# Wide weight pieces spread over the experts' slots: fewer of them in the first ten

## The chip, the cores and the metric

The kernel runs on one NeuronCore of one Trainium2 chip. The metric is the time of one execution on the device in microseconds (us), lower is better. A core has five engines that run their own instruction queues in order and meet at semaphores: the tensor engine (PE) for matrix products, VectorE (DVE), ScalarE (ACT), GpSimd (POOL) and SyncE (SP), which here issues nearly all transfers (DMA). Tiles live in on-chip memory (SBUF), matmul results in PSUM.

## What is computed

Three stages, one after the other, over 1536 tokens of width 512. First attention in 16 heads with a mask by hash buckets, then a mixture of 8 experts in which each token goes to one expert, then a layer with a softmax-like activation and a normalization. The change lies in the second stage and prepares the third:

```python
# experts: every token is computed by the expert e with its largest logit
h = np.maximum(x[mask] @ w1[e], 0.0)          # 512 -> 1024
ye = h @ w2[e]                                # 1024 -> 512
out[mask] = gate_w[mask, None] * eom[mask, e, None] * ye

# last stage
h = x @ w_in                                  # 512 -> 1024
e = np.exp(h - np.max(h, axis=-1, keepdims=True))
solu = h * (e / (np.sum(e, axis=-1, keepdims=True) + 1e-09))
ln = (solu - mu) / np.sqrt(var + 1e-06) * g_ln
out = ln @ w_out                              # 1024 -> 512
```

`w_in` and `w_out` of the last stage arrive as 64-bit floats; all other inputs have 32 bits.

## The kernel before

Every product is computed from 16-bit halves: a number is split into a high half and the rest (low half), and three matmuls (high by high, high by low, low by high) stand for one.

**The expert stage** is a list of 64 slots, written out by the loop over `slots`. A slot is one quarter of one of an expert's two products: 24 matmuls (`mm1` for the first product, `mm2` for the second). The order by blocks of four slots is m1 of expert 0, m1 of 1, m2 of 0, m1 of 2, m2 of 1, m1 of 3, m2 of 2, and so on: m1 of expert e+2 stands behind m2 of expert e. So slots 12 to 15 are m1 of expert 2, 16 to 19 m2 of expert 1, 44 to 47 m1 of expert 6, 60 to 63 m2 of expert 7. The columns of a matmul are the expert's places for tokens: 224, 224, 224, 212, 200, 192, 184, 168 from the fullest expert to the emptiest.

**What is queued in a slot**, in this order: ScalarE makes the high half of one piece of an expert's weights (`w_hi`, L142, 128x1024), VectorE the low half of the piece of the slot before (`w_lo`, L146), SyncE starts the load of the piece three slots ahead (`w_load`, L156 and L158), then whatever the table `todo` holds for the slot, then `run_late`, then the slot's matmuls and their evacuation. Slots 4 to 47 and 52 to 55 have such an expert piece. The raw pieces go through five buffers (`raw`), which VectorE's low half frees. In the third slot of an m1 block SyncE also issues the transposing load of a later expert's tokens (`x_load`, L1037).

**Evacuation.** After m1, ScalarE writes the hidden values twice (L1115, L1117) and GpSimd subtracts (L1118, `hh<-hf,hh`). After every second m2 slot ScalarE writes the high half of `yT` (L1147) and VectorE the low half (L1148); the latter is queued by `run_late` in the next slot, behind that slot's `todo`. PSUM has four buffers for these results (`ps_a`): a slot of m1 takes one, two slots of m2 share one. Each is given back by the instructions that evacuate it, for m2 by L1148.

**The wide pieces.** The 64-bit weights of the last stage come in 16 pieces of 512 KB, 0 to 7 from `w_in`, 8 to 15 from `w_out`. The kernel has no 64-bit arithmetic, so it decodes a piece with integer instructions, 128x512 each. `wide_a` has ScalarE's L122 and VectorE's L123, L125 and L126; `wide_b` is VectorE's L131; then ScalarE makes the high half (L142, `wi` or `wo`) and VectorE the low half (L146). The table `WD` names the slot of `wide_a` for each piece; `wide_b`, the high and the low half follow one, two and three slots later. The first five pieces are loaded before the stage, the others are issued by SyncE three slots ahead of `wide_a` (L110). They share five buffers (`raww`), and the decoded values two (`db`).

**The last stage** takes 12 tiles of 128 tokens: `h2` (L1262, 24 matmuls), then VectorE's and ScalarE's work of `solu_a` to `solu_d`, and four tiles later `outp` (L1329). What `todo` still holds for slots 64 and up is emitted here, two slots for each tile, ahead of that tile's work.

Of the kernel before, what the change touches and what calls it, by code (L numbers as in the profile page):

```python
# [21 lines left out]
def kernel(  # L22
# [903 lines left out]
    with tc.manual_schedule():  # L926
# [259 lines left out]
                f(*a)  # L1186


        WD = [0, 2, 4, 6, 8, 14, 20, 26] + [37 + 4 * x for x in range(8)]
        for x in range(16):  # L1190
            i = WD[x] if wide else 3 + 3 * x
            if wide:
# [16 lines left out]
        for i, (kd, e, g) in enumerate(slots):  # L1209
# [18 lines left out]
            if kd == "m2" and 4 * e + g < NTILE:  # L1228
# [4 lines left out]
                x = nc.gpsimd.indirect_dma_start(  # L1233
                    out=meta[:, :], out_offset=bass.IndirectOffsetOnAxis(ap=po, axis=0),
                    in_=me[:, t], in_offset=None).ins
# [150 lines left out]
```

## Time and profile before

| | before |
|---|---|
| median of 3 runs | 554.01 us |
| lowest and highest | 552.87 and 557.27 us |
| the profiled execution | 556.92 us, its span 555.1 us |
| mean granted clock of the tensor engine | 0.985 |
| PE busy | 518.3 us (93%) |
| VectorE busy | 395.9 us (71%) |
| ScalarE busy | 342.0 us (62%) |
| GpSimd busy | 257.7 us (46%) |
| expert stage, first to last slot | about 264 to 416 us of the span |

The span runs from the first to the last instruction. Busy time is the time in which an engine has an instruction under way. Matmuls are pipelined, so a busy tensor engine is not one at its peak. Averages over the span hide the stage that the change touches: the rows below are read there.

### The profile page before, as it was taken

What the parts mean: (1) busy time and instruction counts of PE and PEld (TensorE: products, weight loads), DVE (VectorE), ACT (ScalarE), POOL (GpSimd) and SP (SyncE); (2) the same over time, 40 slices, a digit from 0 to 9 for tenths busy, and PEclk for the clock granted to TensorE, in tenths of its full rate; (3) what the DMA queues carried; (4) which work ended last, traced back from release to release, by engine and by line L of the source; (5) the groups of instructions that cost most, each with busy time, mean ns of one, the idle gap of its engine ahead of it and who ended that gap; (6) DMA issues with size and microseconds to landing.
All of it is one profiled execution on the core that took longest, in us unless ns stands there. A gap on an engine that the chain in (4) does not pass through costs nothing. (4 is left out here: it accounts for less than half of the span.)

```text
span 555.1 us, 10812 instructions
## 1 busy us (share of the span) xinstructions
PE 518.3 (93%) x3900; PEld 351.5 (63%) x3900; DVE 395.9 (71%) x893; ACT 342.0 (62%) x642; POOL 257.7 (46%) x324
## 2 busy tenths in 40 slices
PE   6789999999999999999997989988999899999993
PEld 5446566666656655667996979987994344444441
DVE  7757777777777787766799987689995875645620
ACT  6677777877867777863386766587643453433420
POOL 7949493939696764716147546232220011121122
PEclk9999999999999999999998989998999999999998
DMA  5584977654839244304777999999600244243271
GB/s 170 109 222 105 225 151 221 151 155 103 230 82 222 90 92 132 91 1 170 234 219 144 330 225 262 235 341 342 243 3 2 43 85 100 58 89 83 57 113 58
DMA packets 107177, 83.13 MB, mean 150 GB/s; under 512 B 80624, under 2 KB 89456, under 8 KB 107120
## 3 DMA queue, kind: packets, MB, share of 16 engines
q1 hardware_dynamic: 104816, 76.09, 53.3%
q0 software_dynamic: 2304, 6.31, 3.2%
q8 instruction: 32, 0.52, 0.4%
q14 instruction: 25, 0.20, 0.1%
HBM read 51.43 MB, written 9.97 MB: 111 GB/s over the span
## 5 line engine op out<-in xcount | busy, mean ns | idle before, releaser
L566 ACT ACTIVATE p<-s,mx 128x768 f32<-128x768 f32 x96 | 95.2, 992 | 51.1 <-DVE mx L555 42.1
L551 DVE TENSOR_REDUCE mx<-s 128x1 f32<-128x768 f32 x96 | 91.7, 955 | 47.9 <-PE s L541 45.9
L580 PE MATMUL t<-ident,p 128*128 128x128 f32 x576 | 124.9, 274 | 0.7 <-ACT pt L582 0.7
L582 ACT COPY pt<-t 128x384 f32<-128x384 f32 x192 | 84.6, 478 | 10.8 <-PE t L580 9.5
L580 PEld LDWEIGHTS t<-ident,p 128*128 128x128 f32 x576 | 77.8, 141 | 15.3 <-ACT pt L582 5.0
L599 PE MATMUL v<-pt,v 128*64 128x384 f32 (+1 forms) x384 | 80.1, 503 | 0.9 <-DVE xt L626 0.9
L1118 POOL TENSOR_TENSOR hh<-hf,hh 128x448 f16<-128x448 f32 (+5 forms) x32 | 40.2, 1259 | 80.1 <-ACT hf L1117 80.1
L1262 PE MATMUL h<-wi,yT 128*128 128x512 f16 x288 | 65.8, 386 | 4.2 <-DVE so L1288 2.6
L1107 PE MATMUL a<-xw,wa 128*128 128x224 f16 (+5 forms) x224 | 57.3, 259 | 9.8 <-DVE yT L1148 8.8
L1138 PE MATMUL a<-hh,wb 128*128 128x224 f16 (+5 forms) x256 | 63.7, 252 | 0.0
L1139 PE MATMUL a<-hh,wb 128*128 128x224 f16 (+5 forms) x256 | 63.6, 251 | 0.0
L1140 PE MATMUL a<-hh,wb 128*128 128x224 f16 (+5 forms) x256 | 63.5, 251 | 0.0
L1329 PE MATMUL o<-wo,zT 128*128 128x512 f16 x288 | 63.5, 379 | 0.0
L541 PE MATMUL s<-k,q 128*128 128x384 f16 x192 | 58.3, 330 | 4.1 <-ACT p L566 4.1
L541 PE MATMUL s<-b,cm 128*128 128x384 f16 x192 | 57.2, 326 | 2.3 <-DVE b L510 1.1
L1109 PE MATMUL a<-xw,wa 128*128 128x224 f16 (+5 forms) x224 | 57.5, 260 | 1.4 <-DVE wa L146 1.4
L1108 PE MATMUL a<-xw,wa 128*128 128x224 f16 (+5 forms) x224 | 57.4, 259 | 0.0
L1262 PEld LDWEIGHTS <-yT 128*128 128x128 f16 x288 | 28.2, 99 | 40.3 <-DVE so L1288 3.8
L1329 PEld LDWEIGHTS <-zT 128*128 128x128 f16 x288 | 28.2, 98 | 34.0
L541 PEld LDWEIGHTS <-q 128*128 128x128 f16 x192 | 19.0, 99 | 39.7 <-issue 37.7
L1277 ACT ACTIVATE ex<-h,st,csc 128x1024 f32<-128x1024 f32 x12 | 14.4, 1203 | 43.3 <-DVE st L1300 32.6
L1301 POOL TENSOR_TENSOR st<-st,nhalf 128x2 f32<-128x2 f32 x12 | 8.5, 707 | 68.6 <-DVE st L1300 68.6
(255 smaller groups left out, 1017.7 us busy)
## 6 DMA issues: line engine op xcount, KB each, us to landing
raw<-in_moe_w_dram SPq DMA_DIRECT2D x64, 512.0 KB, 5.8
raww<-in_moe_w_in_dram SPq DMA_DIRECT2D x8, 512.0 KB
raww<-in_moe_w_out_dram SPq DMA_DIRECT2D x8, 512.0 KB, 6.9
xs<-raw SPq DMA_DIRECT2D x8, 448.0 KB
v<-in_v_dram SPq DMA_DIRECT2D x8, 384.0 KB
q<-in_q_dram SPq DMA_DIRECT2D x7, 384.0 KB, 3.8
k<-in_k_dram SPq DMA_DIRECT2D x7, 384.0 KB, 5.5
cm<-q SPq DMA_DIRECT2D x14, 96.0 KB, 2.1
```

The costliest lines, as they stand in the source:

```text
L541: nc.tensor.matmul(t[:, c, 0:SB], d[x, h][:, s], flat(d[y, h])[:, c * SB:(c + 1) * SB], start=first, stop=not first)
L551: nc.vector.tensor_reduce(out=mx[:, 0:1], in_=t[:, :, 0:SB], op=ALU.max, axis=AX.XY)
L566: nc.scalar.activation(out=p, in_=s_t.pop(i)[:, :, 0:SB], func=AF.Exp, scale=mx[:, 1:2], bias=mx[:, 2:3], accum_out=sums[j][:, qt, h:h + 1])
L580: nc.tensor.transpose(t[:, g * 128:(g + 1) * 128], p[:, c, g * 128:(g + 1) * 128], ident)
L582: nc.scalar.copy(out=pt[j, h][:, 3 * c:3 * c + 3, qt * 128:(qt + 1) * 128], in_=t[:, 0:SB].rearrange("p (g c) -> p g c", g=3))
L599: nc.tensor.matmul(pv[j, q0][64 * h:64 * h + 64, 0:w], vt[:, h, c], pt[j, h][:, c, q0 * 128:q1 * 128], start=(c == 0), stop=(c == NS - 1), ...
L1109: nc.tensor.matmul(ps[:, i, 0:n], w[:, 1, kk, fs], xw[:, kk], start=False, stop=(kk == KD - 1))
L1138: nc.tensor.matmul(ps, w[:, 0, f, ds], hh[:, 0, f], start=(f == 0), stop=False)
L1139: nc.tensor.matmul(ps, w[:, 0, f, ds], hh[:, 1, f], start=False, stop=False)
L1140: nc.tensor.matmul(ps, w[:, 1, f, ds], hh[:, 0, f], start=False, stop=(f == KF - 1))
L1262: nc.tensor.matmul(ps[:, c], yT[:, a, kk, ts], w_i[:, w, kk, c * 512:(c + 1) * 512], start=(kk == 0 and a == 0 and w == 0), stop=(kk == KD ...
L1329: nc.tensor.matmul(ps, zT[:, KF * a + f], w_o[:, w, f], start=(f == 0 and a == 0 and w == 0), stop=(f == KF - 1 and a == 1))
```

## The change

The table that gives each wide piece its slot is replaced. The old one has the first parts of pieces 0 to 7 at slots 0, 2, 4, 6, 8, 14, 20 and 26 and those of 8 to 15 at every fourth slot from 37 to 65. The new one has them at 0, 2, 10, 14, 18, 22, 26 and 30, and then at every fourth slot from 35 to 63. Nothing else differs.

```diff
-        WD = [0, 2, 4, 6, 8, 14, 20, 26] + [37 + 4 * x for x in range(8)]
+        WD = [0, 2, 10, 14, 18, 22, 26, 30] + [35 + 4 * x for x in range(8)]
```

The instructions of the tensor engine and of GpSimd keep their order. On VectorE, in slots 5 to 8 of the program before, the low halves of expert 2's first weights (`wa<-raw,wa`) alternate with the parts of pieces 1 to 4 (`raww` is a raw wide piece, `db` and `dm` its decoded values, `wi` the weights of the last stage):

```order
L146 SCALAR_TENSOR_TENSOR wa<-raw,wa 128x1024
L146 SCALAR_TENSOR_TENSOR wi<-db,wi 128x512
L131 SCALAR_TENSOR_TENSOR db<-dm,db 128x512
L146 SCALAR_TENSOR_TENSOR wa<-raw,wa 128x1024
L123 TENSOR_SCALAR db<-raww 128x512
L125 SCALAR_TENSOR_TENSOR db<-raww,db 128x512
L126 SCALAR_TENSOR_TENSOR db<-raww,db 128x512
L146 SCALAR_TENSOR_TENSOR wa<-raw,wa 128x1024
L146 SCALAR_TENSOR_TENSOR wi<-db,wi 128x512
L131 SCALAR_TENSOR_TENSOR db<-dm,db 128x512
L146 SCALAR_TENSOR_TENSOR wa<-raw,wa 128x1024
L123 TENSOR_SCALAR db<-raww 128x512
```

VectorE's queue after the change, from slot 6 to slot 12 (x5 is five low halves in a row, those of slots 6 to 10):

```order
L146 SCALAR_TENSOR_TENSOR wa<-raw,wa 128x1024 x5
L123 TENSOR_SCALAR db<-raww 128x512
L125 SCALAR_TENSOR_TENSOR db<-raww,db 128x512
L126 SCALAR_TENSOR_TENSOR db<-raww,db 128x512
L1148 ISA
L1148 SCALAR_TENSOR_TENSOR yT<-a,yT 128x2x224
L146 SCALAR_TENSOR_TENSOR wa<-raw,wa 128x1024
L131 SCALAR_TENSOR_TENSOR db<-dm,db 128x512
L146 SCALAR_TENSOR_TENSOR wa<-raw,wa 128x1024
```

Piece 2 now stands in slot 10, between the fifth of these low halves and the first `yT` of expert 0. Later, from slot 43 to 45 of the program before, VectorE's queue has no wide piece ahead of the second `yT` of expert 4 (the one with 200 columns) but a low half:

```order
L146 SCALAR_TENSOR_TENSOR wa<-raw,wa 128x1024 x2
L146 SCALAR_TENSOR_TENSOR wo<-db,g_90,wo 128x512
L1148 ISA
L1148 SCALAR_TENSOR_TENSOR yT<-a,yT 128x2x200
L146 SCALAR_TENSOR_TENSOR wb<-raw,wb 128x1024
L123 TENSOR_SCALAR db<-raww 128x512
```

In the changed program the same place of VectorE's queue, slots 43 to 45, reads:

```order
L146 SCALAR_TENSOR_TENSOR wa<-raw,wa 128x1024
L123 TENSOR_SCALAR db<-raww 128x512
L125 SCALAR_TENSOR_TENSOR db<-raww,db 128x512
L126 SCALAR_TENSOR_TENSOR db<-raww,db 128x512
L146 SCALAR_TENSOR_TENSOR wa<-raw,wa 128x1024
L131 SCALAR_TENSOR_TENSOR db<-dm,db 128x512
L1148 ISA
L1148 SCALAR_TENSOR_TENSOR yT<-a,yT 128x2x200
L146 SCALAR_TENSOR_TENSOR wb<-raw,wb 128x1024 x2
```

The first two parts of piece 10 have moved ahead of that `yT`. At the start of the last stage, VectorE's queue before the change (`st`, `so` and `ex` are the statistics, the activation and the exponential of a tile, `h` the tile's product in PSUM):

```order
L146 SCALAR_TENSOR_TENSOR wo<-db,g_90,wo 128x512
L123 TENSOR_SCALAR db<-raww 128x512
L125 SCALAR_TENSOR_TENSOR db<-raww,db 128x512
L126 SCALAR_TENSOR_TENSOR db<-raww,db 128x512
L1274 TENSOR_REDUCE st<-h 128x1
L1275 SCALAR_TENSOR_TENSOR st<-st,csc 128x1
L1284 TENSOR_SCALAR st<-st 128x1
L1285 RECIPROCAL st<-st 128x1
L1286 TENSOR_TENSOR st<-st,csc 128x1
L1288 SCALAR_TENSOR_TENSOR so,st<-h,st,ex 128x1024
L1290 TENSOR_SCALAR st<-st 128x1
L131 SCALAR_TENSOR_TENSOR db<-dm,db 128x512
```

And after it:

```order
L131 SCALAR_TENSOR_TENSOR db<-dm,db 128x512
L1274 TENSOR_REDUCE st<-h 128x1
L1275 SCALAR_TENSOR_TENSOR st<-st,csc 128x1
L1284 TENSOR_SCALAR st<-st 128x1
L1285 RECIPROCAL st<-st 128x1
L1286 TENSOR_TENSOR st<-st,csc 128x1
L1288 SCALAR_TENSOR_TENSOR so,st<-h,st,ex 128x1024
L1290 TENSOR_SCALAR st<-st 128x1
L146 SCALAR_TENSOR_TENSOR wo<-db,g_90,wo 128x512
```

Piece 14's low half and piece 15's first part have left the stage; piece 15's second part stands ahead of the first tile and its low half ahead of the second, where the second part was.

## Rows read from the trace of the kernel before

**Rows 1.** Timeline of PE: start us, us, instruction, in brackets wait and releaser

```profile
283.58 0.26 PE L1138 MATMUL a<-hh,wb 128*128 128x224 f16 x1
...
292.78 0.26 PE L1107 MATMUL a<-xw,wa 128*128 128x224 f16 x1
...
301.24 0.26 PE L1107 MATMUL a<-xw,wa 128*128 128x224 f16 x1 [2.07 <-DVE yT L1148]
...
307.55 0.26 PE L1138 MATMUL a<-hh,wb 128*128 128x224 f16 x1
...
325.58 0.25 PE L1107 MATMUL a<-xw,wa 128*128 128x212 f16 x1 [2.13 <-DVE yT L1148]
...
363.88 0.24 PE L1107 MATMUL a<-xw,wa 128*128 128x192 f16 x1 [1.80 <-DVE yT L1148]
...
380.58 0.24 PE L1107 MATMUL a<-xw,wa 128*128 128x184 f16 x1 [2.52 <-DVE yT L1148]
...
386.09 0.25 PE L1138 MATMUL a<-hh,wb 128*128 128x192 f16 x1
```

**Rows 2.** PE's waits, 270 to 460: total us, times, longest

```profile
PE a L1107 <- DVE yT L1148: 8.8, 5, 2.5
...
PE a L1109 <- DVE wa L146: 1.4, 1, 1.4
```

**Rows 3.** Stretches: length, busy us of each engine, granted clock, DMA share, GB/s

```profile
303.00:304.00 1.00, 1.00 (x8) 0.80 (x6) 1.00 (x2) 0.73 (x3) 0.36 (x1) 0.50 1.90 137
...
363.80:366.00 2.20, 2.12 (x26) 2.12 (x26) 1.30 (x4) 2.20 (x4) 0.32 (x1) 1.00 1.03 385
```

**Rows 4.** Stretches of DVE alone: length, busy, granted clock, DMA share, GB/s

```profile
292.80:316.80 24.00, 22.79 (x25) 0.93 0.90 237
366.40:385.20 18.80, 18.63 (x20) 0.91 1.02 329
```

**Rows 5.** Timeline of DVE in the expert stage

```profile
272.72 0.43 DVE L123 TENSOR_SCALAR db<-raww 128x512 int32<-128x512 int32 x1 [3.34 <-DMA raw<-in_moe_w_dram]
...
376.44 0.41 DVE L123 TENSOR_SCALAR db<-raww 128x512 int32<-128x512 int32 x1
376.89 0.69 DVE L125 SCALAR_TENSOR_TENSOR db<-raww,db 128x512 int32<-128x512 int32 x1
...
378.22 1.22 DVE L146 SCALAR_TENSOR_TENSOR wa<-raw,wa 128x1024 f16<-128x1024 f32 x1
...
383.38 0.56 DVE L1148 SCALAR_TENSOR_TENSOR yT<-a,yT 128x400 f32 x1
...
385.20 1.14 DVE L123 TENSOR_SCALAR db<-raww 128x512 int32<-128x512 int32 x1
```

**Rows 6.** DVE's waits, 272.7 to 385.3

```profile
DVE db L123 <- DMA raww<-in_moe_w_in_dram: 5.9, 3, 2.9
DVE wa L146 <- ACT wa L142: 4.2, 4, 2.6
...
DVE wb L146 <- ACT wb L142: 2.8, 3, 1.6
```

**Rows 7.** The chain that ended last: start us, us, what

```profile
427.95 0.60 DVE db L131
...
435.48 0.66 DVE wo L146
...
453.46 5.18 PE h L1262 x24
```

**Rows 8.** Timelines of POOL and of DVE at the same time

```profile
272.94 2.54 POOL L1118 TENSOR_TENSOR hh<-hf,hh 128x448 f16<-128x448 f32 x2 [9.88 <-ACT hf L1117]
...
273.18 1.40 DVE L125 SCALAR_TENSOR_TENSOR db<-raww,db 128x512 int32<-128x512 int32 x1
```

**Rows 9.** Timelines of ACT and of PE at the handover

```profile
415.70 0.72 ACT L142 ACTIVATE wo<-db,g 128x512 f16<-128x512 f32 x1 [2.59 <-DVE db L131]
...
441.24 7.04 PE L1262 MATMUL h<-wi,yT 128*128 128x512 f16 x24 [2.15 <-DVE so L1288]
```

## The prediction, made before the change was run

> **What bounds the kernel now.** I read three views, in this order: the tensor engine's waits over the expert stage, its timeline there, and VectorE's timeline beside it. A slot is 24 matmuls of one expert, numbered 0 to 63 as in the loop; at 224 columns four slots without a wait take 283.58 to 292.78, so one takes 2.30 us [rows 1]. The tensor engine is the stage's work, and what it loses is lost from the end. It waits 8.8 us, in five places, for the low half of `yT` (L1148) and 1.4 us for the low half of an expert weight (L146), and both come from VectorE [rows 2]. The places are slots 14, 23, 31, 39 and 46: each needs a PSUM buffer that the `yT` instruction queued four or three slots earlier gives back. Slot 14 starts after a wait of 2.07 us, and slots 14 and 15 together then take from 301.24 to 307.55, 6.31 us and not 4.60 [rows 1]. The missing 1.7 us is the clock: granted at 0.50 between 303 and 304, that is 1.2 GHz, after the engine had stood still for 2.07 us. After the 1.80 us wait before 363.88 the clock stayed at 1.00, 2.4 GHz [rows 1, 3]. So a long wait costs itself and 1.7 us more; I count three such places, before 301.24, 325.58 and 380.58.
>
> Why is VectorE late? From 292.8 to 316.8 it is busy 22.8 of 24.0 us, and from 366.4 to 385.2 18.6 of 18.8 us [rows 4]. Between these it stops: 5.9 us for three transfers of wide weights, 4.2 and 2.8 us for ScalarE's high halves of expert weights, 12.9 us in all between 272.72, its first wide instruction, and 385.20 [rows 5, 6]. So it is overfull in slots 2 to 16, has rests from slot 16 to 36, and is full again from slot 37.
>
> **The change, part by part.** It adds and removes no instruction. A wide piece x costs VectorE the three instructions of its first part (376.44 to 378.22, 1.78 us), 0.60 us a slot later, and 0.66 two slots after that, as piece 15 shows: 3.0 us [rows 5, 7]. Pieces 2, 3 and 4 go from slots 4, 6, 8 to 10, 14, 18; pieces 5, 6, 7 from 14, 20, 26 to 22, 26, 30; pieces 8 to 15 come two slots earlier.
>
> First, slots 4 to 9. Three pieces, 9 us of VectorE, leave the queue ahead of the weight that slot 12 waits for and of the `yT` of slot 10. Its first part now stands right ahead of that `yT`, but the 7 us taken off before it are more. I expect the 1.4 us at slot 12 and the 2.07 + 1.7 us at slots 14 and 15 to go.
>
> Second, slots 10 to 48. Now every eight slots hold two pieces, eight low halves of expert weights and two `yT`. That mix stands in the trace already: 366.4 to 385.2, 18.8 us, of which VectorE is busy 18.63 [rows 4]. Eight slots of the tensor engine take 18.4 us at 224 columns and fewer as the experts get smaller. So VectorE loses a little on it from slot 12, more later, and at the end of this stretch it sets the time: slot 47 needs the second `yT` of slot 44, which ended at 383.38 + 0.56 = 383.94 [rows 5]. I work out that one instruction. From 272.72 to 385.20 VectorE had 112.5 - 12.9 = 99.6 us of work. In the changed order the queue up to that `yT` holds, beside this, piece 10's first two parts (1.78 + 0.60 = 2.4 us), and not the one weight half that followed it (1.22 us): 100.8 us. It ends at 272.72 + 100.8 + I = 373.5 + I, where I is VectorE's rest. **I is the unknown.** No row shows it for this order. Below, it is 0 (the full stretch of rows 4 has 0.2 us in 18.8); above, it is 12.9, as before, if the transfers stay as late as they were. I take 5, nearer to the row with the same mix, and not less because the expert weights come through five buffers that VectorE itself frees. That gives 378.5, 5.4 us earlier than 383.94. From there to slot 48 before took 2.15 us (383.94 to 386.09) [rows 1]; a slot of 184 columns is 2.30 x 184 / 224 = 1.89 us. Since VectorE is now the later engine, slot 47 may begin with a long wait again; half a chance of 1.7 us makes it 1.89 + 0.85 = 2.74. Net gain at slot 48: 5.4 - 0.6 = 4.8 us.
>
> Of VectorE's work much is contention with GpSimd: the same instruction (L125) took 1.40 us at 273.18, beside GpSimd's two subtractions from 272.94 on, and 0.69 us at 376.89 [rows 5, 8]. Each GpSimd subtraction so cost some 0.7 us, and that is in the 99.6. The Trainium skill, "SBUF — State Buffer", section "Who interferes with whom", says that a VectorE instruction with two SBUF inputs and a GpSimd instruction that reads SBUF share a port, and that the later one blocks for the whole of the other. The trace agrees only in part: 0.71 us was lost beside an instruction of 1.27 us (half of the 2.54). At full length, 0.56 us more on each of some 26 such subtractions up to slot 47, an estimate by that page, the sum would be 14 us longer.
>
> Third, slots 48 to 63: no low halves of expert weights but four; the tensor engine bound there and stays so. Cost nothing, covered by VectorE's free time; without it, one piece is 3.0 us.
>
> Fourth, the handover. ScalarE's last `yT` copy stood behind piece 14's high half, which began at 415.70 after 2.59 us of waiting for VectorE and took 0.72 [rows 9]. Piece 14 is now two slots earlier: 0.7 us gained. Piece 15's first part now lies ahead of the last `yT`, but it fits in the last two slots' matmuls.
>
> Fifth, the start of the last stage. The chain that ended last runs there through VectorE, with piece 15's two parts in it, 0.60 us at 427.95 and 0.66 us at 435.48 [rows 7]. One part moves under the first tile's matmuls, the other takes the first one's place: 0.6 us gained. The wait before 441.24 shrinks from 2.15 to 1.5 us, under the 1.80 that kept the full clock. Those 24 matmuls took 7.04 us, later ones 5.18 [rows 7, 9]; the 1.86 us would go too. I count half of it, 0.9.
>
> **Sum.** 4.8 + 0.7 + 0.6 + 0.9 = 7.0 us. The profiled execution took 556.92 us, 2.9 above the median of the three runs, so its waits may be somewhat larger than usual; I take the sum from the median, 554.0 - 7.0 = 547.0, and forecast 547.
>
> **Rivals.**
> *VectorE never rests:* I = 0, and the clock stays up: 10.4 + 0.3 + 0.7 + 0.6 + 1.9 = 13.9 us, 540. For it: the dense stretch. Against it: five weight buffers, with a transpose among the transfers. Chance 0.15.
> *The work has only moved:* VectorE's total is what it was and the rests come back as waits for expert weights, I = 10 to 12.9. The `yT` of slot 44 then ends 0.4 us earlier to 2.5 later, and with the handover the kernel takes 553 to 557. GpSimd's contention belongs here: should each of the 26 subtractions cost a third more than its 0.7 us, 0.25, the gain shrinks by 6.5 us, to 553.5. For it: VectorE stood still for the wide transfers in each of the three pieces that had room. Chance 0.23.
> *Wide transfers hold the queue (slower):* before, pieces 5, 6 and 7 waited 2.0 us each in VectorE's queue. Now pieces 5 to 10 are all loaded three slots ahead of their decoding while expert weights flow. If all six wait 2.0 us, and ScalarE's 7.0 us stay, I is 19: 8.6 us later at slot 47, which with the clock and the handover makes 561. It turns to a loss from I = 12. Against it: pieces 9 and 10 ran in the dense stretch without a wait, because the queue was late anyway. Chance 0.10.
> Forecast: 0.52, from 542 to 551.
>
> **How the numbers follow.** Two runs of this kernel differ by up to 4 us, so 1% (5.5 us) is about what can be told from no change. Faster by more than 1% is under 548.5: the first rival and 0.7 of the forecast, 0.15 + 0.36 = 0.51. Within 1%: 0.16 + 0.23 = 0.39. Slower: 0.10. The range reaches from just above the best case to the second rival's end, 541 to 556; it leaves out the slower rival and a part of the best.
>
> **What would show it.** Right: slots 12 to 15 without a wait or a half clock; slot 16 near 302 where it was 307.6; VectorE without a rest over 1 us between slots 10 and 48; the remaining waits at slots 39 and 47, for `yT`; the last stage starting 5 to 6 us earlier. Wrong: rests of VectorE for wide transfers in pieces 6 to 10; waits at slots 22 and 23 as long as before; a sum of VectorE's busy time that grew by more than 3 us.

## The result, and the profile after

| | before | after |
|---|---|---|
| median | 553.56 us (9 runs, 550.80 to 557.27) | 548.57 us (9 runs, 546.21 to 551.43) |
| ratio to before, 95% interval | | 0.9916, 0.9891 to 0.9942 |
| the profiled execution | 556.92 us | 548.64 us |
| its span, mean granted clock | 555.1 us, 0.985 | 546.9 us, 0.989 |

The change gains 5.0 us, 0.84% by the ratio: less than the 1% that the prediction set as its bound for faster, though the interval lies wholly below 1. 547 was forecast, with 541 to 556 around it. The times and the profile do not give the same amount: the two profiled executions lie 8.3 us apart, since that of before is 3.4 us above the median of its runs and that of after is at its median.

The page of after, busy time of each engine:

```profile
PE 514.4 (94%) x3900; PEld 349.9 (64%) x3900; DVE 397.0 (73%) x893; ACT 341.9 (63%) x642; POOL 263.4 (48%) x324
```

VectorE (DVE) has as much work as before in total: 397.0 against 395.9 us. What changed is when it does it. PE's waits of after from 262 to 460 (total us, times, longest), to be read beside [rows 2]:

```profile
PE a L1107 <- DVE yT L1148: 6.6, 4, 4.1
```

Five waits for `yT` are now four, 8.8 us are 6.6, and the 1.4 us for `wa` (L1109) have no row any more. Where they stand is read in PE's timeline of after (start us, us, instruction, in brackets the wait and who ended it):

```profile
264.39 0.26 PE L1107 MATMUL a<-raw,wa 128*128 128x224 f16 x1 [0.71 <-ACT raw L875]
...
302.41 0.26 PE L1138 MATMUL a<-hh,wb 128*128 128x224 f16 x1
...
320.33 0.26 PE L1138 MATMUL a<-hh,wb 128*128 128x224 f16 x1
...
337.21 0.25 PE L1107 MATMUL a<-xw,wa 128*128 128x200 f16 x1 [1.19 <-DVE yT L1148]
...
352.82 0.24 PE L1107 MATMUL a<-xw,wa 128*128 128x192 f16 x1 [0.71 <-DVE yT L1148]
...
359.04 0.32 PE L1107 MATMUL a<-xw,wa 128*128 128x192 f16 x1 [4.08 <-DVE yT L1148]
...
364.69 0.25 PE L1138 MATMUL a<-hh,wb 128*128 128x200 f16 x1
...
378.36 0.24 PE L1107 MATMUL a<-xw,wa 128*128 128x184 f16 x1 [0.59 <-DVE yT L1148]
...
380.25 0.25 PE L1138 MATMUL a<-hh,wb 128*128 128x192 f16 x1
```

The same timeline of before, at slots 0 and 24, which [rows 1] does not have (the second still at half clock, after the wait at slot 23):

```profile
263.99 0.26 PE L1107 MATMUL a<-raw,wa 128*128 128x224 f16 x1 [0.71 <-ACT raw L875]
...
329.03 0.39 PE L1138 MATMUL a<-hh,wb 128*128 128x224 f16 x1
```

Counted from slot 0, so that the 0.4 us later start drops out:

| | before | after | gained so far |
|---|---|---|---|
| to slot 16 | 307.55 - 263.99 = 43.56 | 302.41 - 264.39 = 38.02 | 5.5 |
| to slot 24 | 329.03 - 263.99 = 65.04 | 320.33 - 264.39 = 55.94 | 9.1 |
| to slot 48 | 386.09 - 263.99 = 122.10 | 380.25 - 264.39 = 115.86 | 6.2 |

So 9.1 us are gained by slot 24, and 2.9 of them are given back by slot 48, at slots 31, 38, 39 and 47. These sizes belong to the two profiled executions. Two other profiles run the changed program's instructions up to slot 48 (r_after and e3_nobranch, below): they need 117.6 and 117.2 us to slot 48 and not 115.9, so against the one profile of before the gain there was 4.5 to 6.2 us. The largest wait is at slot 39: 4.08 us, and behind it matmuls of 0.32 to 0.37 us, where the same shape took 0.24, up to 364.69. Stretches of after show both sides (length, then busy us of PE, PEld, DVE, ACT, POOL, then the granted clock, DMA share, GB/s):

```profile
293.20:311.60 18.40, 18.40 (x194) 18.40 (x193) 18.30 (x19) 12.58 (x21) 15.49 (x16) 1.00 0.97 226
...
348.00:364.70 16.70, 11.91 (x111) 11.11 (x109) 15.67 (x19) 13.67 (x22) 4.76 (x4) 0.80 0.99 322
...
276.00:386.00 110.00, 102.38 (x1103) 100.98 (x1101) 106.49 (x111) 81.82 (x128) 59.19 (x50) 0.97 1.02 287
```

The first is the place of the old waits at slots 12 to 15: PE busy all 18.4 us, clock 1.00. The second holds slot 39, clock 0.80. The third is nearly the whole stage: VectorE is busy 106.5 of 110 us there. The same stretch of before:

```profile
276.00:386.00 110.00, 98.77 (x1028) 96.04 (x1026) 95.95 (x102) 78.54 (x122) 51.07 (x48) 0.95 0.95 262
```

VectorE's rest in it went from 14.0 to 3.5 us, and 111 instructions fit where 102 did. What is left of the rests stands in VectorE's timeline of after, with the two `yT` that slots 39 and 47 wait for:

```profile
343.13 0.43 DVE L123 TENSOR_SCALAR db<-raww 128x512 int32<-128x512 int32 x1 [1.59 <-DMA raww<-in_moe_w_in_dram]
...
354.86 0.43 DVE L123 TENSOR_SCALAR db<-raww 128x512 int32<-128x512 int32 x1 [0.96 <-DMA raww<-in_moe_w_out_dram]
...
358.40 0.59 DVE L1148 SCALAR_TENSOR_TENSOR yT<-a,yT 128x424 f32 x1
...
377.74 0.56 DVE L1148 SCALAR_TENSOR_TENSOR yT<-a,yT 128x400 f32 x1
```

Both rests are for a transfer of a wide piece. SyncE issues all of these loads (start us, us that the issue took). The first row is the load that the first rest waited for; then come a transposing load of tokens (L1037) and the load of `mr` (L1241), with the load of an expert weight (L156) behind:

```profile
331.87 0.47 SPq L110 DMA_DIRECT2D raww<-in_moe_w_in_dram  x1
...
339.08 0.35 SPq L156 DMA_DIRECT2D raw<-in_moe_w_dram  x1
339.55 4.61 SPq L1037 DMA_TRANSPOSE xw<-xs  x1
344.28 1.26 SPq L1241 DMA_DIRECT2D mr<-meta  x1
345.79 3.20 SPq L156 DMA_DIRECT2D raw<-in_moe_w_dram  x2
```

Piece 7's load was thus issued 7.7 us ahead of the transposing load and landed only 11.2 us after its issue, where the 512 KB loads of expert weights took 6.2 us (median from 330 to 360): it was slow in transfer, not held in SyncE's queue. The expert weight at 345.79 was held there, and the load of piece 8, issued at 349.03, stood behind it.

At the handover and the start of the last stage, PE of after:

```profile
410.67 1.55 PE L1262 MATMUL h<-wi,yT 128*128 128x512 f16 x5 [0.63 <-ACTq L1067]
413.01 14.63 PE L1262 MATMUL h<-wi,yT 128*128 128x512 f16 x67 [0.79 <-issue]
...
435.00 5.35 PE L1262 MATMUL h<-wi,yT 128*128 128x512 f16 x24 [1.49 <-DVE so L1288]
```

and of before, whose later row is in [rows 9]:

```profile
416.86 1.40 PE L1262 MATMUL h<-wi,yT 128*128 128x512 f16 x5 [1.17 <-ACTq L1067]
418.66 1.25 PE L1262 MATMUL h<-wi,yT 128*128 128x512 f16 x5 [0.40 <-issue]
```

PE falls still 2.97 us before the second of these rows in both kernels (410.67 - 0.63 = 410.04 to 413.01, and 416.86 - 1.17 = 415.69 to 418.66): nothing is gained at the handover. The last stage restarts 418.66 - 413.01 = 5.65 us earlier. From there to the fifth tile it takes 21.99 and not 22.58 us, and that tile's 24 matmuls 5.35 and not 7.04 us: 0.59 and 1.69 us more. 5.65 + 0.59 + 1.69 = 7.9 of the 8.2 us by which the spans differ.

### The profile page after: what moved, and what is told of

The parts are those of the page before. It is cut to its first block, busy times and chain, and to the rows that moved or that the text cites. A ratio compares the mean times of both kernels' runs of the same rounds, so it can differ in the third digit from the quotient of the medians.

```text
span 546.9 us, 10807 instructions
## 1 busy us (share of the span) xinstructions
PE 514.4 (94%) x3900; PEld 349.9 (64%) x3900; DVE 397.0 (73%) x893; ACT 341.9 (63%) x642; POOL 263.4 (48%) x324
## 5 line engine op out<-in xcount | busy, mean ns | idle before, releaser
L582 ACT COPY pt<-t 128x384 f32<-128x384 f32 x192 | 84.8, 479 | 11.2 <-PE t L580 9.9
L1118 POOL TENSOR_TENSOR hh<-hf,hh 128x448 f16<-128x448 f32 (+5 forms) x32 | 43.5, 1371 | 65.5 <-ACT hf L1117 65.5
L1262 PE MATMUL h<-wi,yT 128*128 128x512 f16 x288 | 64.2, 379 | 3.5 <-DVE so L1288 2.0
L1107 PE MATMUL a<-xw,wa 128*128 128x224 f16 (+5 forms) x224 | 56.0, 253 | 7.6 <-DVE yT L1148 6.6
L1109 PE MATMUL a<-xw,wa 128*128 128x224 f16 (+5 forms) x224 | 56.1, 254 | 0.0
L1108 PE MATMUL a<-xw,wa 128*128 128x224 f16 (+5 forms) x224 | 56.1, 254 | 0.0
```

The costliest lines, as they stand in the source:

```text
L582: nc.scalar.copy(out=pt[j, h][:, 3 * c:3 * c + 3, qt * 128:(qt + 1) * 128], in_=t[:, 0:SB].rearrange("p (g c) -> p g c", g=3))
L1108: nc.tensor.matmul(ps[:, i, 0:n], w[:, 0, kk, fs], xw[:, KD + kk], start=False, stop=False)
L1262: nc.tensor.matmul(ps[:, c], yT[:, a, kk, ts], w_i[:, w, kk, c * 512:(c + 1) * 512], start=(kk == 0 and a == 0 and w == 0), stop=(kk == KD ...
```

## Experiments

All are edits of the changed kernel. Ratios are to the kernel before, run beside them: the first four experiments shared its runs, and so did the next four and the last three. Each run's profile is of one execution. The theory at the start: the gain comes from the pieces taken out of slots 4 to 9 and from the `yT` waits at slots 14 and 23; the later pieces, two slots earlier each, give part of it back.

### The two halves of the change apart

The early half alone, the later pieces where they were (e1_early):

```diff
-WD = [0, 2, 10, 14, 18, 22, 26, 30] + [35 + 4 * x for x in range(8)]
+WD = [0, 2, 10, 14, 18, 22, 26, 30] + [37 + 4 * x for x in range(8)]
```

> Only pieces 2 to 7 move; 8 to 15 stay at 37 to 65. Theory (VectorE's queue sets the tensor engine's waits): slots 12 to 15 without a wait, as in the changed kernel. Without pieces 8 to 10 two slots earlier, the yT of slot 36 and of slot 44 stand behind 2.4 us less of VectorE's work, so the wait of 4.08 us at slot 39 shrinks under 2 us and keeps the full clock (2.7 us), and slot 48 starts 2 to 5 us earlier than in the changed kernel. At the start of the last stage piece 15's two parts are back in the chain: 0.6 us more, and the half clock before the fifth tile, 1.7 us. In all 545 to 549 us, a ratio to before of 0.985 to 0.993. Rival (the gain comes from pieces 8 to 15 being two slots earlier): 552 to 554, a ratio over 0.997.

Measured: 549.43 us, ratio 0.9896 (0.9874 to 0.9918), as much as the whole change. Its PE waits, and its row at the fifth tile of the last stage:

```profile
PE a L1107 <- DVE yT L1148: 5.6, 6, 1.4
```

```profile
432.50 7.04 PE L1262 MATMUL h<-wi,yT 128*128 128x512 f16 x24 [2.15 <-DVE so L1288]
```

No wait is over 1.4 us, the clock stays at 1.00 from slot 0 to slot 47, and slot 48 stands 112.4 us behind slot 0, 3.5 us better than in the changed kernel's profile. The last stage gives 2.3 us of this back: its fifth tile waits 2.15 us and runs at half clock again, exactly as before the change. How much of the 3.5 us the table earns is open: e9_mix, below, runs the same instructions up to slot 48 and needed 116.6 us for them.

The late half alone (e2_late):

```diff
-WD = [0, 2, 10, 14, 18, 22, 26, 30] + [35 + 4 * x for x in range(8)]
+WD = [0, 2, 4, 6, 8, 14, 20, 26] + [35 + 4 * x for x in range(8)]
```

> Only pieces 8 to 15 move two slots earlier; 0 to 7 stay. Theory: waits and half clock at slots 12 to 15 and 23 as before; piece 10's first two parts ahead of the yT of slot 44 put slot 47 up to 2.4 us later; the last stage's start gains 0.6 us and the half clock before its fifth tile, 1.7 us. In all 551 to 555 us, a ratio of 0.996 to 1.003. Rival (the gain comes from these pieces): 548 to 549, a ratio of 0.99 to 0.993.

Measured: 556.67 us, ratio 1.0029 (1.0006 to 1.0051). PE's waits, and its row at slot 39:

```profile
PE a L1107 <- DVE yT L1148: 13.5, 6, 3.3
...
PE a L1109 <- DVE wa L146: 1.5, 1, 1.5
```

```profile
366.75 0.24 PE L1107 MATMUL a<-xw,wa 128*128 128x192 f16 x1 [2.98 <-DVE yT L1148]
```

The waits at slots 12, 14 and 23 are there again (1.48, 2.08 and 3.33 us). Slot 39 waits 2.98 us where it waited 1.80 before the change, and slot 47 3.23 where slot 46 waited 2.52. So the early half makes the gain; the late half costs some 3 us in the expert stage (125.1 us to slot 48, 122.1 before) and earns its 2.3 us (0.59 + 1.69) at the start of the last stage.

### The handover

The loop for overflowing tokens left out (e3_nobranch):

```diff
         run_late()
-        overflow()
```

> The changed kernel without the loop for tokens over an expert's places (these inputs have none, so it runs zero times). In both kernels the tensor engine has its pause 3.13 us after slot 63's matmuls behind it, whatever piece 14 does. If the branch around that loop makes the pause: the last stage's matmuls run on without a break some 1 us after slot 63, and the kernel is 1.5 to 2.5 us shorter than the changed one (546 to 547). If the pause comes from VectorE's or ScalarE's last pieces: within 0.5 us of the changed kernel.

Measured: 548.81 us, ratio 0.9880 (0.9854 to 0.9905). PE, and the DMA queues from 409.5 to 415.5 (packets, MB, share):

```profile
411.30 0.24 PE L1140 MATMUL a<-hh,wb 128*128 128x168 f16 x1
411.37 15.70 PE L1261 MATMUL h<-wi,yT 128*128 128x512 f16 x72
```

```profile
q14 instruction: 1, 0.01, 0.4%
```

The same rows of the changed kernel from 408 to 414:

```profile
q8 instruction: 1, 0.02, 1.4%
q14 instruction: 1, 0.01, 0.5%
```

Without the loop the 72 matmuls follow the last expert matmul without a pause and end 427.07 - 411.54 = 15.53 us after its end. With it they end 427.64 - 410.04 = 17.60 us after that point, where PE fell still. So the loop that runs zero times, its branch (L1067) included, costs 2.1 us here, and it goes with a transfer of instructions on queue 8 that is absent without it. The interval of the time overlaps that of the changed kernel, so the 2.1 us rest on the trace. ScalarE's wait for piece 14's decoding, the prediction's cause, was not what PE paused for.

### What fills VectorE

GpSimd's subtraction replaced (e4_memset):

```diff
-            late.append(lambda: nc.gpsimd.tensor_tensor(out=hh[:, 1, 2 * g:2 * g + 2], in0=hf, in1=o,
-                                                        op=ALU.subtract))
+            late.append(lambda: nc.gpsimd.memset(hh[:, 1, 2 * g:2 * g + 2], 0.0))
```

> The changed kernel with GpSimd's subtraction of the hidden values' low half replaced by writing zeros there (the low halves of the hidden values are left out), an instruction that reads nothing. Theory (each subtraction costs VectorE 0.7 us): the doubled instructions of VectorE are gone (L126 0.69 us everywhere), its work up to the yT of slot 44 is some 17 us less, the tensor engine has no wait for yT in slots 12 to 63 and keeps the full clock: 1.2 + 0.7 + 4.1 + 0.6 us of waits and 2.7 us of half clock, so 9 us less than the changed kernel, 538 to 541. Rival (contention is not what fills VectorE): within 2 us of the changed kernel, 547 to 549. If VectorE is held through any GpSimd instruction, the same.

Measured: 546.69 us, ratio 0.9844 (0.9810 to 0.9879): 4 us better than the changed kernel by the ratios, between the 9 of the theory and the 2 of the rival. VectorE's groups from 270 to 386, of the changed kernel (busy us, mean ns):

```profile
L146 DVE SCALAR_TENSOR_TENSOR wb<-raw,wb 128x1024 f16<-128x1024 f32 x19 | 28.3, 1496 | 0.0
...
L126 DVE SCALAR_TENSOR_TENSOR db<-raww,db 128x512 int32<-128x512 int32 x12 | 9.7, 811 | 0.4
```

and with the memset, with VectorE's longest rest for a wide load, PE's row of its longest wait behind it, and a row of GpSimd and one of VectorE beside it:

```profile
L146 DVE SCALAR_TENSOR_TENSOR wa<-raw,wa 128x1024 f16<-128x1024 f32 x24 | 29.2, 1221 | 11.0 <-ACT wa L142 10.8
L146 DVE SCALAR_TENSOR_TENSOR wb<-raw,wb 128x1024 f16<-128x1024 f32 x20 | 24.2, 1216 | 0.2 <-ACT wb L142 0.2
...
L126 DVE SCALAR_TENSOR_TENSOR db<-raww,db 128x512 int32<-128x512 int32 x12 | 8.3, 692 | 0.4
```

```profile
335.31 0.43 DVE L123 TENSOR_SCALAR db<-raww 128x512 int32<-128x512 int32 x1 [3.18 <-DMA raww<-in_moe_w_in_dram]
```

```profile
337.78 0.32 PE L1107 MATMUL a<-xw,wa 128*128 128x200 f16 x1 [2.77 <-DVE yT L1147]
```

```profile
293.71 1.98 POOL L1118 MEMSET hh<- 128x448 f16 x4 [17.61 <-PE a L1139]
...
294.54 0.73 DVE L123 TENSOR_SCALAR db<-raww 128x512 int32<-128x512 int32 x1
```

Each VectorE instruction falls to about its shortest time: all twelve of L126 take 691 to 693 ns, where the changed kernel has 691 to 1408. Over the eight groups of that stretch, each count times the difference of the means, this is about 20 us of VectorE in the changed kernel, and 16 us by the same sum before the change. The Trainium skill, "SBUF — State Buffer", section "Who interferes with whom", says that a VectorE instruction with two inputs in SBUF contends with a GpSimd instruction that reads SBUF and not with one that only writes there; the trace agrees for these, 811 ns beside subtractions and 692 ns beside memsets. It is otherwise for L123, which has one input: beside the four memsets above it took 0.73 and not 0.42 us. But with 20 us of work gone, PE still waits, and the stage up to slot 48 takes 112.7 us, only 3.2 less than in the changed kernel. VectorE's rests are back, 10.8 us for ScalarE's high halves and 3.18 us for one wide load, and it is the loads that come late: ScalarE itself waits 17.4 us there for raw weights of the first product, 5.8 in the changed kernel. VectorE's work and the transfers are two limits at about the same height.

### Can the loads be had earlier?

Wide loads six slots ahead and not three (e5_load6):

```diff
-put(i - 3, wide_load, x, dec)
+put(i - 6, wide_load, x, dec)
```

> The changed kernel with the wide pieces' loads issued six slots ahead of their decoding and not three. Theory (VectorE's rests there, 1.6 us for piece 7 and 1.0 us for piece 8, are late transfers): both rests go, the yT of slot 36 ends 2.5 us earlier, the 4.1 us wait at slot 39 falls under 2 us and its half clock (2.7 us) goes too: 2 to 5 us less than the changed kernel, a ratio to before of 0.982 to 0.988. Rival (the transfers' order only moves the rest): the expert weights' transfers come later, VectorE rests for ScalarE's high halves instead, and the kernel stays within 1 us of the changed one, 0.990 to 0.994.

Measured: 551.71 us, ratio 0.9945 (0.9917 to 0.9973). The rests for wide loads are gone; one of 3.9 us for an expert weight stands in their place, and slot 39 waits longer than in any other run:

```profile
339.21 8.38 SPq L1037 DMA_TRANSPOSE xw<-xs  x1
```

```profile
361.79 0.32 PE L1107 MATMUL a<-xw,wa 128*128 128x192 f16 x1 [7.33 <-DVE yT L1148]
```

The transposing load now held SyncE for 8.38 us, and ScalarE waited 4.33 us for a raw expert weight queued behind it. Here the rival was right that the rest only moves, and it became longer.

The second part of `yT` ahead of the other work of its slot (e7_ytfirst):

```diff
+            run_late()
             if prep[i]:
                 each(w_hi, prep[i])
...
             for f, a in todo.pop(i, []):
                 f(*a)
-            run_late()
```

> The changed kernel with the late half of yT (and GpSimd's subtraction) queued at the head of the next slot, ahead of that slot's expert weight half and wide piece. Theory (the tensor engine waits for what stands ahead of yT in VectorE's queue, not for VectorE's total): every yT ends 1.1 to 3.0 us earlier against VectorE's work, so the waits at slots 31, 38, 39 and 47 (6.6 us) shrink by 1.1 to 1.7 us each and the half clock of 2.7 us may go: 3 to 6 us less than the changed kernel, 0.980 to 0.986. Rival (VectorE's total sets the stage): within 1 us of the changed kernel, 0.990 to 0.994.

Measured: 552.16 us, ratio 0.9952 (0.9925 to 0.9979); the waits for `yT` are 9.2 us in six places, 4.80 at slot 39, where three executions of the changed program's expert stage waited 4.08, 5.10 and 5.82. Its place in the slot did not shorten the wait.

### Combinations

The early half's spacing in the expert stage and an end like the changed kernel's (e9_mix):

```diff
-WD = [0, 2, 10, 14, 18, 22, 26, 30] + [35 + 4 * x for x in range(8)]
+WD = [0, 2, 10, 14, 18, 22, 26, 30] + [37, 41, 45, 49, 53, 57, 60, 63]
```

> Pieces 0 to 7 as in the changed kernel, 8 to 13 as before (37 to 57), 14 and 15 at 60 and 63. Theory: the expert stage of the run with only the early pieces moved (slot 48 some 3.4 us earlier than in the changed kernel) and the start of the last stage of the changed kernel (full clock, 0.6 us shorter): 2 to 4 us less than the changed kernel, a ratio of 0.984 to 0.988. If it stays at 0.990 or above, the two gains are not separate.

Measured: 549.94 us (547.79 to 554.30), ratio 0.9904 (0.9871 to 0.9938). Its profiled execution was its longest, with 9.8 us of `yT` waits in six places; the gains of the two halves did not add up. Two things stand behind this. Up to slot 48 the instructions are those of e1_early, and VectorE is busy the same 106 us; yet this execution took 116.6 us and that one 112.4. The transposing load of slot 30 held SyncE for 6.18 us here and 3.43 there. That is how far two executions of one order lie apart, so a single profile does not rank these tables. And at the handover ScalarE's last `yT` copy now stands behind the parts of pieces 14 and 15 (PE's rows):

```profile
412.24 1.04 PE L1262 MATMUL h<-wi,yT 128*128 128x512 f16 x4 [1.68 <-ACTq L1067]
414.38 1.03 PE L1262 MATMUL h<-wi,yT 128*128 128x512 f16 x2 [1.10 <-DVEq L1067]
```

PE restarts 3.82 us after it fell still and not 2.97, and at half clock, so that it takes 25.17 us to the fifth tile and not 21.99.

This table, the loads of e5_load6 and the order of e7_ytfirst together (e10_all):

> The table of the run before this one, with the wide loads six slots ahead and yT's low half at the head of the slot. Theory: the three add up where they are not the same wait: no wait over 1.5 us in slots 12 to 63, no half clock, slot 48 near 374 of the span: 8 to 11 us less than the changed kernel, a ratio of 0.972 to 0.979. If VectorE's total sets the stage: not under 0.983.

Measured: 554.62 us, ratio 0.9986 (0.9962 to 1.0011). A clear miss: together they undo the gain. Slot 48 stands at 379.81, no worse than in the changed kernel, but at the handover PE waits for ScalarE's queue:

```profile
414.54 1.89 PE L1262 MATMUL h<-wi,yT 128*128 128x512 f16 x4 [3.60 <-ACTq L1067]
```

Its pause there is 5.74 us, and the way to the fifth tile takes 24.22 us, the first of it at half clock: 5.0 us more than in the changed kernel, of 6.2 by which the spans differ.

### Slot 39

The last group shared another chip. First the changed kernel once more, as its own reference (r_after):

> The changed kernel once more, as the measure for the two runs beside it on the same chip: a ratio to before of 0.989 to 0.994 as in the first measurement. If it lies above 0.995, the gain depends on the chip or the hour.

Measured: 551.14 us, ratio 0.9921 (0.9892 to 0.9950). Slot 39 waited 5.10 us in this profile and slot 47 1.81, where the first had 4.08 and 0.59: executions of the same kernel differ just there.

Then the transposing loads of experts 4 to 7 one slot later and `mr` four slots later (e11_sp):

```diff
-if g == 2 and kd == "m1" and e + 2 < E:
+if g == (3 if e > 1 else 2) and kd == "m1" and e + 2 < E:
...
-if i == 30:
+if i == 34:
```

> The changed kernel with the transposing load of the experts 4 to 7 one slot later (behind that slot's expert weight) and the 12 KB load of the tokens' places (mr) at slot 34 and not 30. Theory (the 4.1 us wait at slot 39 comes from SyncE, which is held for 4.6 us by the transposing load of slot 30 and 1.3 us by mr, so that the expert weight whose buffer was free at 339.1 is only loaded at 345.8): that weight is loaded some 5 us earlier, the next one 2 us later than its buffer is free; VectorE's rest at piece 8 and the wait at slot 39 fall under 1.5 us, no half clock there: 3 to 6 us less than the changed kernel, 0.981 to 0.986. Rival (VectorE's total sets slot 47 whatever happens at 39): slot 48 not more than 1.5 us earlier than in the changed kernel, a ratio above 0.988.

Measured: 549.09 us, ratio 0.9894 (0.9859 to 0.9929). VectorE's 1.59 us rest, piece 7's, is gone, and piece 8's has grown from 0.96 to 1.87 us, behind these rows of SyncE:

```profile
342.48 5.10 SPq L1037 DMA_TRANSPOSE xw<-xs  x1
347.83 0.37 SPq L156 DMA_DIRECT2D raw<-in_moe_w_dram  x1
348.24 0.43 SPq L110 DMA_DIRECT2D raww<-in_moe_w_out_dram  x1
```

```profile
358.59 0.32 PE L1107 MATMUL a<-xw,wa 128*128 128x192 f16 x1 [4.04 <-DVE yT L1148]
```

Slot 39 waits as long as ever. And the same with the table of e9_mix (e12_spmix):

> The same two moves on the table with pieces 8 to 13 as before (37 to 57) and 14, 15 at 60 and 63. Theory: less of VectorE's work ahead of slots 39 and 47 as well, so 1 to 3 us less than the run before this one, 0.976 to 0.983. Rival: as that run, 0.988 or above.

Measured: 548.88 us, ratio 0.9891 (0.9858 to 0.9924). Slot 39 waits 0.63 us, but slot 46 now waits 3.02, and the half clock follows there:

```profile
372.66 0.24 PE L1107 MATMUL a<-xw,wa 128*128 128x184 f16 x1 [3.02 <-DVE yT L1148]
```

None of these tables and orders is told apart from the changed kernel: e1_early, e9_mix, e11_sp and e12_spmix lie between 0.989 and 0.991, the changed kernel at 0.992 in both groups.

## Why the prediction was right, and where it was not

**The early slots: right.** 1.4 us at slot 12 and 3.8 us at slots 14 and 15 were to go; the trace gains 5.5 us by slot 16, without a wait or a half clock, and slot 16 stands at 302.41 where 302 was said. e1_early and e2_late show that pieces 2 to 7 do it; no run moved 2 to 4 alone, but 5 to 7 stood, from slot 14 on, behind the `yT` of slot 10 that slot 14 waited for. Another 3.6 us came by slot 24, the wait and half clock of slot 23; the prediction had no row of its own for them, they were in its sum for slot 48.

**The expert stage to slot 48: the result right, one of its parts not.** The second `yT` of slot 44 was put at 378.5 and ends at 377.74 + 0.56 = 378.30. But it was put there with a rest I of 5 us. The rests are 1.59 + 0.96 = 2.55 us, half of that, and the stage began 0.4 us late; 373.5 + 0.4 + 2.6 = 376.5, so 1.8 us more of VectorE's work stand in the queue than I took over from before. Contention with GpSimd more than covers them: taking each instruction of the queue from 272.72 to this `yT` at what it took beyond the mean of its form in e4_memset, the sum is 15.3 us before and 18.1 after. The prediction had written the contention of the old order into its 99.6 us as if it were fixed. Two misses of about 2 us cancelled, and that was luck. The 14 us that it worked out for contention at full length had no room: of the expert weights' low halves from 270 to 386, 1.21 us at the shortest, none took over 2.08 us in either kernel. Of the 5.84 us by which slot 48 is earlier, 4.8 were forecast; most of the rest is the half clock at slot 47, for which I had counted half a chance: the wait there is 0.59 us and the clock stayed up. That VectorE would have no rest over 1 us between slots 10 and 48 failed at one place, the 1.59 us before piece 7.

**Where the waits would be: right in the main.** Slots 39 and 47, for `yT`; slots 31 and 38 have 1.9 of the 6.6 us, which was not said. That slot 39 alone would take 4.08 us and a half clock after it was not said either. VectorE's full queue is shown as one cause by e4_memset, where slot 39 waits 1.02 us; that the transfers are another is shown by e5_load6, which lengthened the wait to 7.33 us. e11_sp moved the rest from piece 7 to piece 8 and left the wait as it was. How many of the 4.08 us belong to which is open: no run took away one of the two and left the other as it was.

**The handover: wrong.** 0.7 us were to come from piece 14's high half, which stood ahead of ScalarE's last `yT` copy. That copy now follows the last expert matmul at once and PE's first wait is 0.63 and not 1.17 us, but the second wait grew from 0.40 to 0.79 and the restart is 2.97 us behind in both. e3_nobranch shows what sets it: the overflow loop with its branch. The step that failed took the wait nearest to the handover for the one that sets it. The mechanism itself exists: in e9_mix, e10_all and e12_spmix, with pieces 14 and 15 at 60 and 63, ScalarE's last copy comes later still, and the pauses are 3.82, 5.74 and 3.46 us.

**The start of the last stage: right, and undersized.** 0.6 us for the part of piece 15 that moves: 0.59 measured. For the half clock ahead of the fifth tile I took 0.9, half of 1.86, since the wait of 1.5 us lay below the 1.80 that had kept the clock. The wait is 1.49, the clock stayed up, and the term is 1.69: the row was to be believed in full. e1_early, with 2.15 us there and 7.04 us of matmuls behind it, is the counterpart.

**The sum against the median: wrong by 2 us.** 7.0 us were worked out from the profiled execution and then taken from the median, although the text noted that this execution lay 2.9 us above it and that its waits may be larger than usual. On the profiled executions the change gains 8.3 us, more than the sum; on the medians 5.0. r_after shows where executions of one kernel differ, the waits at slots 39 and 47 with the clock behind them; what differed between executions of the kernel before was not seen, since one was profiled. The gain of 0.84% fell in the class within 1%, to which 0.39 was given, and the range of 541 to 556 would have held no change as well.

**The rivals.** VectorE without any rest was nearly reached (3.5 us of rest in 110), and yet the time was not 540: the work itself grew, and one half clock stayed. That the work only moves took part: 2.9 us of 9.1 came back at slots 31 to 47. Wide transfers that hold the queue, the slower case, showed as 2.55 us and not 12. Rests for wide transfers in pieces 6 to 10 were named as a sign of being wrong, and pieces 7 and 8 had them; they were too small to take the gain. e5_load6 shows that they can cost more than they do here.

## What to carry to other kernels

When work is spread away from a place where an engine is overfull, ask what the engine's total is on the new path up to the last instruction that someone waits for, contention included: once it has no rests left, moving a piece or a load only chooses the slot that waits. One long wait can cost a stretch at half clock besides itself. Profile the same order more than once before ranking spacings: the same instructions up to slot 48 took 112.4 us in one execution and 116.6 in another. And a gain read from one profiled execution is to be shrunk when that execution lies above its median.

## What the runs showed of the hardware

- A loop that runs zero times, with the branch past it, stopped PE for 2.1 us (17.60 against 15.53 us to the end of the same 72 matmuls), with a transfer of instructions beside it that is absent without the loop.
- One and the same transposing load held SyncE's queue for 3.43 us (e1_early), 4.61 (after), 5.10 (e11_sp), 5.17 (r_after), 6.18 (e9_mix) and 8.38 us (e5_load6), and loads queued behind it were issued that much later. A wide load that was issued 7.7 us ahead of it still took 11.2 us to land.
- GpSimd's subtractions lengthened VectorE's instructions by some 20 us between 270 and 386. With memsets in their place no two-input instruction that the text names was longer than its shortest (L126 691 to 693 ns); the one-input L123 took 0.73 and not 0.42 us beside four memsets.
- In the expert stage PE's clock, where it stood at 2.4 GHz, stayed there after each wait of up to 1.81 us, and matmuls at 1.2 GHz followed most longer ones: those of 2.52 and 2.53, 2.77, 3.02 to 3.33 and 4.04 to 7.33 us. Between, and once above, it went either way: it fell after 2.07 and 2.13 [rows 1] and 2.14 us (e10_all), and stayed after 2.05 and 2.10 (e9_mix), 2.08 and even 2.98 us (e2_late, granted clock 1.00 behind it). At the handover of e9_mix it fell to 0.50 after two waits of 1.68 and 1.10 us with four matmuls between them.
